# Attention over inducing points and a gated product in one kernel: coefficients without a clip, the first group of x in one load, and another order of all operations

## The chip, the cores and the metric

One Trainium2 chip, one core. The metric is the device time of one execution in microseconds (us). TensorE (PE) multiplies, VectorE (DVE) and ScalarE (ACT) read its results from PSUM and write to SBUF, GpSimd (POOL) works in SBUF and issues the loads that change the type, SyncE (SP) issues the other transfers.

## The reference

```python
# x: (4, 12480, 128), inducing: (32, 128), w_in: (128, 2048), w_out: (2048, 128)
def mab(q, kv):
    s = scale * (q @ kv.transpose(0, 2, 1))          # scale = 1 / sqrt(128)
    s = s - s.max(-1, keepdims=True)
    a = np.exp(s)
    a /= a.sum(-1, keepdims=True) + 1e-09
    return a @ kv
h = mab(I, x)                       # per batch: 32 rows out of 12480
y = mab(x, h)                       # per batch: 12480 rows, each a mixture of the 32 rows of h
u = y.reshape(49920, 128) @ w_in
out = (u * np.clip(u + 3.0, 0.0, 6.0) / 6.0) @ w_out
```

## The kernel before

Each row of y is a mixture of 32 rows of h, so u is a mixture of the 32 rows of h @ w_in, and, where no u leaves -3 to 3, the result is a quadratic form in the 32 weights. The kernel computes the coefficients of this form once for each batch and then needs, for each row of x, products of two weights with these coefficients. At the end a verdict is counted that the assumptions held; where it fails, a slow direct path runs. With these inputs it does not run.

A batch has six groups of 2048 rows (16 tiles of 128) and a small one of 192 rows. Everything up to the verdict is a list of short operations, written out by hand in one table, ORDER. A token there is an operation's code, then batch, group and details, and at the end often the PSUM bank and the engine (V, A or P for VectorE, ScalarE, POOL). The function runs through the tokens and issues the instructions of each on its engine. Engines and queues work in the order of the table, each for itself, and wait for each other where data or buffers demand it.

The operations that the text names:

- X loads a group of x (fp32 in HBM, fp16 in SBUF; issued by POOL; seven buffers xh). T transposes 8 tiles on TensorE, Y copies the result to SBUF (xT). S are the scores against the inducing rows, E their exponentials (a), A the sums over rows on TensorE, H adds them to hacc on VectorE.
- When hacc of a batch is complete: c3 spreads the denominator on TensorE, c4 inverts it, c9, cK, cA, cB make HS and Wd (h and differences of its rows), c7 and c8 split hacc in two bf16 parts, G multiplies by w_in on TensorE (w_in itself split in w_hi and w_lo by wh and wl), cG scales to GL. cD copies GL to Gd in bf16 (two halves). Then, for the coefficients of single weights, cH and cI, L with w_out, cL, cm and cN, cM; for the products of pairs, p (a 128x2048 product, PR) and P with w_out in bf16 (wb); cP, cX and cY bring the coefficients into place (Cq).
- For each group: Z are TensorE's products of xT with HS and Wd, Zz and Zd take them out of PSUM (z, and dk by an exponential), Ze makes e, ee its square, W spreads dk over partitions by a transfer from SBUF to SBUF (d, issued by SP). B spreads z to pairs on TensorE, F takes the exponential (TF, 128x1024), U multiplies TF by d (TD, 128x2048). R, Rr and R2 give the squared normalization. l and q are TensorE's products with the coefficients, v multiplies them by the normalization and writes os, O stores os to HBM (SP).
- wi and wo load w_in and w_out (POOL), i and w are constants and warm-up products at the start. y0 to y3 count for the verdict on VectorE (each count is a pass over a small tile at line 831), y4 sums over partitions on TensorE, y5 makes bad_i, and all engines read bad_i before they end. cJ takes the largest |GL| of a batch for the verdict (g_all), cC and cQ are sums of squares for it on ScalarE.

The lines that the profile names: 416 X, 422 T, 428 Y, 433 S, 441 E, 449 A, 459 A's denominators, 476 H, 481 c3, 402 wh, 405 wl, 532 cG, 540 cD, 543 cH, 548 cI, 553 cJ, 563 L, 609 p, 616 P, 641 cQ, 656 Z, 666 Zd, 671 Ze, 678 Zz, 692 ee, 698 W, 704 R, 731 B, 741 F, 750 U, 770 l, 789 q, 807 and 811 v, 817 O, 831 counts, 854 y4.

Of the kernel before, what the change touches and what calls it, by code (L numbers as in the profile page):

```python
# [183 lines left out]
def kernel(  # L184
# [35 lines left out]
    with ExitStack() as es:  # L220
# [321 lines left out]
        def op_cH(b, e):  # L542
            veng(e).tensor_scalar(
                r6[:, :, :], GL[:, :, :M].bitcast(FP32), 3.0, 0.0, op0=ALU.add, op1=ALU.max
            )
# [485 lines left out]
```

## Time and profile before

| | |
|---|---|
| time, median of 3 runs | 248.84 us (248.77 to 250.02) |
| time of the profiled execution | 249.51 us |
| its span, first to last instruction | 247.5 us |
| mean granted TensorE clock | 0.982 |
| busy: PE, DVE, ACT, POOL | 227.0, 202.4, 191.1, 40.3 us |
| moved by DMA | 53.91 MB |

How to read it: the busy time of an engine is the time in which it worked on an instruction; TensorE's matmuls overlap, so their durations are longer than their distance. The granted clock is the share of full speed that the throttle allowed to TensorE. In a list of groups a row has line, engine, operation, output<-input and count, then busy us and mean ns of one, then the idle time just before and what ended it. In a list of waits it is the engine and line that waited, what it waited for, the sum in us, the times and the longest. A row of the timeline starts with start and length in us. A row of the chain that ended last has start, length, engine, tile and line.

### The profile page before, as it was taken

What the parts mean: (1) busy time and instruction counts of PE and PEld (TensorE: products, weight loads), DVE (VectorE), ACT (ScalarE), POOL (GpSimd) and SP (SyncE); (2) the same over time, 40 slices, a digit from 0 to 9 for tenths busy, and PEclk for the clock granted to TensorE, in tenths of its full rate; (3) what the DMA queues carried; (4) which work ended last, traced back from release to release, by engine and by line L of the source; (5) the groups of instructions that cost most, each with busy time, mean ns of one, the idle gap of its engine ahead of it and who ended that gap; (6) DMA issues with size and microseconds to landing.
All of it is one profiled execution on the core that took longest, in us unless ns stands there. A gap on an engine that the chain in (4) does not pass through costs nothing. (4 is left out here: it accounts for less than half of the span.)

```text
span 247.5 us, 10076 instructions
## 1 busy us (share of the span) xinstructions
PE 227.0 (92%) x4317; PEld 186.5 (75%) x4317; DVE 202.4 (82%) x438; ACT 191.1 (77%) x350; POOL 40.3 (16%) x80
## 2 busy tenths in 40 slices
PE   1879799999799999999899999999999999989990
PEld 0568758888698798797787888888878877768780
DVE  0236879989599997999778998988889999998983
ACT  2167277998788886999687786999889889989870
POOL 8518582021002500010004000000031000000000
PEclk9999679999999999999999999999999999999998
DMA  6999789969989999849879974623981849696953
GB/s 96 193 255 254 238 158 193 208 163 250 214 286 263 277 196 331 293 87 250 184 252 265 266 274 110 224 56 76 338 305 37 262 97 340 211 311 170 362 232 134
DMA packets 23744, 53.91 MB, mean 218 GB/s; under 512 B 3697, under 2 KB 16785, under 8 KB 20753
## 3 DMA queue, kind: packets, MB, share of 16 engines
q1 hardware_dynamic: 19072, 38.36, 47.4%
q0 software_dynamic: 4624, 14.88, 31.0%
q8 instruction: 34, 0.56, 0.8%
q14 instruction: 14, 0.11, 0.1%
HBM read 27.67 MB, written 25.56 MB: 215 GB/s over the span
## 5 line engine op out<-in xcount | busy, mean ns | idle before, releaser
L741 ACT ACTIVATE TF<-ps 128x1024 f16<-128x1024 f32 (+1 forms) x100 | 96.8, 1007 | 16.1 <-PE ps L731 12.4
L750 DVE TENSOR_TENSOR TD<-TF,d 128x2048 f16<-128x2048 f16 (+1 forms) x52 | 59.9, 1156 | 3.0 <-ACT TF L741 2.2
L789 PE MATMUL ps<-Cq,TF 128*128 128x128 f16 (+1 forms) x784 | 57.9, 219 | 2.6 <-issue 1.4
L789 PE MATMUL ps<-Cq,TD 128*128 128x128 f16 (+1 forms) x784 | 56.0, 219 | 0.0
L807 DVE TENSOR_TENSOR os<-ps,r 128x512 f32<-128x512 f32 x68 | 45.4, 683 | 11.7 <-PE ps L789 4.1
L789 PEld LDWEIGHTS <-TF 128*128 128x128 f16 (+1 forms) x784 | 46.3, 98 | 6.3 <-issue 6.0
L789 PEld LDWEIGHTS <-TD 128*128 128x128 f16 (+1 forms) x784 | 46.1, 99 | 4.3 <-issue 3.4
L811 ACT ACTIVATE os<-ps,r 128x128 f32<-128x128 f32 x112 | 32.0, 380 | 4.3 <-PE ps L789 2.0
L422 PE MATMUL ps<-ident_h,xh 128*128 128x128 f16 x384 | 29.8, 226 | 5.5 <-DMA xh<-in_x_dram 5.5
L422 PEld LDWEIGHTS <-xh 128*128 128x128 f16 x384 | 24.0, 102 | 11.6 <-DMA xh<-in_x_dram 7.5
L428 DVE COPY xT<-ps 128x1024 f16<-128x1024 f16 x31 | 21.2, 684 | 12.8 <-PE ps L422 12.5
L428 ACT COPY xT<-ps 128x1024 f16<-128x1024 f16 x17 | 17.0, 1015 | 18.9 <-PE ps L422 18.8
L416 POOL DMA_DIRECT2D xh<-in_x_dram x25 | 13.9, 560 | 75.1 <-PE ps L459 62.2
L731 PE MATMUL ps<-z,pair 32*128 32x256 f16 (+1 forms) x400 | 20.3, 270 | 0.0
L609 DVE TENSOR_TENSOR PR<-Gd 128x2048 bf16<-128x2048 bf16 x16 | 19.8, 1239 | 0.0
L678 DVE TENSOR_SCALAR_CACHE_REDUCE z<-ps 128x512 f16<-128x512 f32 (+1 forms) x28 | 17.3, 621 | 2.4 <-PE ps L656 2.3
L666 ACT ACTIVATE dk<-ps 128x512 f16<-128x512 f32 (+1 forms) x28 | 14.8, 547 | 5.5 <-PE ps L656 3.4
L770 PE MATMUL ps<-BD,ee 64*128 64x256 f16 (+1 forms) x196 | 17.5, 273 | 0.2
L441 ACT ACTIVATE a<-ps 128x512 f16<-128x512 f32 (+1 forms) x27 | 14.6, 556 | 2.6 <-PE ps L433 2.6
L616 PE MATMUL ps<-w_ob,PR 128*128 128x128 bf16 x256 | 16.5, 219 | 0.0
L671 ACT ACTIVATE e<-z 128x512 f16<-128x512 f16 (+1 forms) x28 | 16.3, 589 | 0.1
L616 PEld LDWEIGHTS <-PR 128*128 128x128 bf16 x256 | 14.7, 98 | 0.9 <-issue 0.8
(137 smaller groups left out, 284.8 us busy)
## 6 DMA issues: line engine op xcount, KB each, us to landing
...
xh<-in_x_dram POOLq DMA_DIRECT2D x23, 512.0 KB, 8.8
os<-in_moe_w_in_dram POOLq DMA_DIRECT2D x2, 512.0 KB, 13.4
w_or<-in_moe_w_out_dram POOLq DMA_DIRECT2D x2, 512.0 KB, 11.6
out_dram<-os SPq DMA_DIRECT2D x2, 512.0 KB, 3.6
...
```

Of the source, the lines that this page charges most:

```text
L422: nc.tensor.transpose(pt[:, (i - lo) * p : (i - lo + 1) * p], at(xh, xhl, b, g)[:p, i, :], ident_h[:p, :p])
L428: copier(e)(xT_of(b, g)[:, lo * p : hi * p], ps[:, k, :].bitcast(FP16)[:, : (hi - lo) * p])
L609: veng(e).tensor_mul(pr_of(b, c)[:, :, :].rearrange("p a (i m) -> p a i m", m=M), views[0], views[1])
L616: nc.tensor.matmul(ps[:, k, f * C : (f + 1) * C], lhsT=pr_of(b, c)[:, jb, :], rhs=w_ob[:, jb, :], start=first_of(b, u), stop=False, skip_g ...
L678: nc.vector.tensor_scalar(fat(z_, b, g)[:rows, :w], ps[:rows, k, :w], 1.0, None, op0=ALU.mult, op1=ALU.min, accum_out=z_all[:rows, b * NGR ...
L731: nc.tensor.matmul(ps[:, pairs[j // 2] + j % 2, f * w : (f + 1) * w], lhsT=pair[rows, f, :], rhs=fat(z_, b, g)[rows, h * w : (h + 1) * w], ...
L741: nc.scalar.activation(hat(TF_, b, g, h)[:, 2 * q : 2 * q + 2, :w], ps[:, k : k + 2, :w], ACT.Exp, scale=scale / KH)
L750: nc.vector.tensor_mul(split(hat(TD_, b, g, h)), split(hat(TF_, b, g, h)), d.unsqueeze(2).to_broadcast([P, J, 2, w]),)
L770: nc.tensor.matmul(ps[:p, ks[jp], s2 * 2 * C : (s2 + 1) * 2 * C], lhsT=fat(e2_, b, g)[rows, s * p : (s + 1) * p], rhs=BD_[b % 2][rows, :, ...
L789: nc.tensor.matmul(ps[:p, k, (s2 * 2 + j2) * C : (s2 * 2 + j2 + 1) * C], lhsT=t[:, j, f * w + s2 * p : f * w + (s2 + 1) * p], rhs=Cq_[b % ...
L807: nc.vector.tensor_mul(o, src, r.unsqueeze(3).to_broadcast([p, Sh, 2, C]))
L811: nc.scalar.mul(o[:, s2, j2, :], src[:, s2, j2, :], r[:, s2, j2 : j2 + 1])
```

## The change

- cI no longer clips: cH (r6 = max(GL + 3, 0) on POOL) is gone, and cI computes (GL + 3) * GL in place of min(r6, 6) * GL. The two are the same where |GL| is at most 3, which the verdict demands.
- cJ moves from VectorE to ScalarE: a sum of the squares of GL in a partition and batch, with the bound 9 in y3 in place of the largest magnitude with the bound 3.
- Group 0 of batch 0 comes in one load (it came in two halves), and it is the first load.
- The table ORDER is another one: all operations stand in another order, and several change their engine. 13 of 28 squares ee and 3 of 16 products p go from VectorE to POOL. Of the copies Y, 23 run on ScalarE and 29 on VectorE (19 and 33 before). Eight warm-up products are left of sixteen. The count of z_all (y2) stands earlier, not among the last operations.

```diff
-        r6 = sb.tile([P, FB, M], FP32, name="r6")
...
-        def op_cH(b, e):
-            veng(e).tensor_scalar(
-                r6[:, :, :], GL[:, :, :M].bitcast(FP32), 3.0, 0.0, op0=ALU.add, op1=ALU.max
-            )
-
         def op_cI(b):
             nc.vector.scalar_tensor_tensor(
-                GL[:, :, M:], r6[:, :, :], 6.0, GL[:, :, :M].bitcast(FP32), op0=ALU.min, op1=ALU.mult
+                GL[:, :, M:],
+                GL[:, :, :M].bitcast(FP32),
+                3.0,
+                GL[:, :, :M].bitcast(FP32),
+                op0=ALU.add,
+                op1=ALU.mult,
             )
 
         def op_cJ(b):
-            nc.vector.tensor_reduce(
-                g_all[:, b : b + 1],
+            nc.scalar.activation(
+                junk[:, :].rearrange("p (a m) -> p a m", m=M),
                 GL[:, :, :M].bitcast(FP32),
-                axis=AX.XY,
-                op=ALU.max,
-                apply_absolute_value=True,
+                ACT.Square,
+                accum_out=g_all[:, b : b + 1],
             )
...
-            count(3, g_all[:, :], 3.0, ALU.is_le)
+            count(3, g_all[:, :], 9.0, ALU.is_le)
...
-it X.0.1.0.16 i2 i1 w.2.0 i3.V T.0.1.0.8.1 Y.0.1.0.8.1.V i0 w.2.5 w.2.2 X.0.0.8.16 T.0.0.8.16.1 w.2.7 Y.0.0.8.16.1.V
...
+X.0.0.0.16 i2 w.2.1 w.2.7 X.0.6.0.2 it i1 i8 i0 i4.1 i5.1.V w.2.0 X.0.1.0.16 w.2.0 i3.V T.0.6.0.2.2 T.0.0.0.8.3
...
```

Three places show the order. A row has the line (in the changed kernel two or three less than before), the operation, output<-input with the buffers' own numbers, and the size. First POOL, from the constants at the start to the loads of w_out; xh0 to xh6 are the buffers of x, os1 takes w_in, sel, a1l, z_all and r2 are constants. Before:

```order
L391 DMA os1_118<-in_moe_w_in_dram 128x1024
L416 DMA xh5_73<-in_x_dram 128x2048
L361 MEMSET a1l0_95 128x128
L361 MEMSET a1l1_96 128x128
L362 MEMSET z_all_166 128x28
L363 MEMSET r2_165 128x392
L416 DMA xhl0_75<-in_x_dram 96x256
L391 DMA os1_118<-in_moe_w_in_dram 128x1024
L416 DMA xh0_68<-in_x_dram 128x2048
L416 DMA xh6_74<-in_x_dram 128x2048
L395 DMA w_or_150<-in_moe_w_out_dram 128x1024 x2
```

And now:

```order
L377 MEMSET sel_155 64x640
L381 TENSOR_TENSOR sel_155<-I4_152 32x128 x4
L382 CAST sel_155<-I4_152 32x128
L414 DMA xh5_73<-in_x_dram 128x2048
L359 MEMSET a1l0_95 128x128
L359 MEMSET a1l1_96 128x128
L360 MEMSET z_all_165 128x28
L361 MEMSET r2_164 128x392
L414 DMA xh4_72<-in_x_dram 128x2048
L389 DMA os1_118<-in_moe_w_in_dram 128x1024 x2
L414 DMA xh0_68<-in_x_dram 128x2048
L414 DMA xh6_74<-in_x_dram 128x2048
```

Both halves of w_in now stand behind the last large group of batch 0 (xh4), the small group (xhl0) is the second load of all, and sel is made between the fourth and the fifth large load.

Second VectorE around the end of the first batch's sums: w_hi and w_lo are wh and wl, hacc is H, rD and d_all are c4. Before:

```order
L428 COPY xT5_82<-ps_67 128x1024
L476 TENSOR_TENSOR hacc0_134<-hacc0_134,ps_67 128x33 x2
L402 CAST w_hi_147<-os1_118 128x512 x2
L476 TENSOR_TENSOR hacc0_134<-hacc0_134,ps_67 128x33 x5
L405 TENSOR_TENSOR w_lo_148<-os1_118,w_hi_147 128x512
L490 CAST HTb_139<-hacc0_134 128x32
L493 TENSOR_TENSOR HTl_140<-hacc0_134,HTb_139 128x32
L486 RECIPROCAL rD_136<-ps_67 128x32
```

And now:

```order
L426 COPY xT4_81<-ps_67 128x1024
L400 CAST w_hi_146<-os1_118 128x512
L403 TENSOR_TENSOR w_lo_147<-os1_118,w_hi_146 128x512
L400 CAST w_hi_146<-os1_118 128x512
L474 TENSOR_TENSOR hacc0_134<-hacc0_134,ps_67 128x33 x7
L484 RECIPROCAL rD_136<-ps_67 128x32
L485 COPY d_all_167<-ps_67 128x32
L494 SCALAR_TENSOR_TENSOR HQ_137<-hacc0_134,rD_136 128x64
```

Of the conversions of w_in one w_hi, one w_lo and another w_hi stand ahead of the last seven additions; the two others are on ScalarE, and no conversion stands between the additions and rD.

Third POOL's last operations, in batches 2 and 3: Wd is cB, HTl is c8, r6 is cH, ee and PR are the squares and the products p. Before:

```order
L416 DMA xh6_74<-in_x_dram 128x2048
L416 DMA xh2_70<-in_x_dram 128x2048
L514 TENSOR_TENSOR Wd1_133<-HQ_137 128x32
L493 TENSOR_TENSOR HTl_140<-hacc1_135,HTb_139 128x32
L543 TENSOR_SCALAR r6_143<-GL_141 128x512
```

And now:

```order
L414 DMA xh6_74<-in_x_dram 128x2048
L689 TENSOR_TENSOR ee2_102<-e2_99 128x512
L689 TENSOR_TENSOR ee1_101<-e1_98 128x512
L689 TENSOR_TENSOR ee2_102<-e2_99 128x512
L512 TENSOR_TENSOR Wd1_133<-HQ_137 128x32
L689 TENSOR_TENSOR ee1_101<-e1_98 128x512
L606 TENSOR_TENSOR PR0_121<-Gd_142 128x2048
L606 TENSOR_TENSOR PR2_123<-Gd_142 128x2048
L689 TENSOR_TENSOR ee1_101<-e1_98 128x512
L689 TENSOR_TENSOR ee0_100<-e0_97 128x512 x2
L689 TENSOR_TENSOR ee1_101<-e1_98 128x512
L689 TENSOR_TENSOR ee2_102<-e2_99 128x512
```

The clip is gone, and behind the last load of x POOL now has nine squares and two products of pairs (p.3.0 into PR0, p.3.2 into PR2).

More of the change, by code (lines that the diff above doesn't have):

```diff
@@ new lines @@
+T.1.5.0.8.7 T.1.5.8.16.6 cY.0.0.3.A W.0.1.3 Y.1.4.8.16.4.A X.1.6.0.2 R.0.2.2 R2.0.1.V Rr.0.3.0 Y.1.5.0.8.7.A
+q.0.0.0.1.0.3 W.0.1.0 U.0.0.0 q.0.0.0.0.1.0 q.0.0.0.1.1.3 l.0.0.0.0.3 l.0.0.1.7.1 X.2.1.0.16 ee.0.3.P Y.1.5.8.16.6.V
+Zd.0.4.5 W.0.3.0 W.0.2.1 R2.0.0.V v.0.0.0.1.3.A Rr.0.2.2 T.1.6.0.2.4 Y.1.6.0.2.4.A q.0.0.1.0.1.7 U.0.1.0 q.0.0.0.0.0.0
+v.0.0.0.0.0.A T.1.2.8.16.6 q.0.0.1.1.0.1 W.0.2.2 B.0.1.1.2.4 F.0.1.1.1.4 F.0.1.1.0.2 v.0.0.1.1.1.V Y.1.2.8.16.6.V
+q.0.0.1.0.0.7 T.1.2.0.8.0 Y.1.2.0.8.0.V q.0.1.0.1.0.1 q.0.1.0.1.1.1 v.0.0.1.0.7.V R2.0.3.V ee.0.1.P W.0.3.3 U.0.1.1
@@ new lines @@
+B.0.3.1.2.6 O.0.0.0.16 Ze.0.5 l.0.2.0.5.4 v.0.2.0.1.4.V W.0.4.1 F.0.3.1.1.6 W.0.4.3 l.0.2.1.1.0 q.0.2.1.1.1.0
+q.0.2.1.0.0.1 q.0.2.1.0.1.1 S.1.4.0.16.6 F.0.3.1.0.2 X.2.6.0.2 v.0.2.0.0.5.V v.0.2.1.0.1.V U.0.3.0 E.1.4.0.16.6
+S.1.5.0.16.7 E.1.5.0.16.7 q.0.2.1.1.0.0 A.1.6.0.2.4 H.1.6.0.2.4 A.1.4.0.16.1 H.1.4.0.16.1 W.0.4.2 T.2.1.8.16.6
+A.1.5.0.16.4 v.0.2.1.1.0.A U.0.3.1 H.1.5.0.16.4 c7.1.V B.0.4.0.2.0 F.0.4.0.0.2 q.0.3.0.1.1.5 c3.1.4 q.0.3.0.0.0.7
+q.0.3.0.0.1.7 ee.0.4.V c4.1.4 Y.2.1.8.16.6.V W.0.5.0 c9.1 R.0.4.2 Rr.0.4.2 F.0.4.0.1.0 cK.1 q.0.3.0.1.0.5 W.0.4.0
@@ new lines @@
+U.0.4.0 l.0.3.1.6.4 l.0.3.0.7.5 c8.1.V B.0.4.1.0.2 cQ.0 F.0.4.1.1.2 R2.0.4.V X.2.0.0.16 O.0.1.0.16 v.0.3.0.0.7.V
+X.3.6.0.2 q.0.3.1.1.1.4 F.0.4.1.0.0 q.0.3.1.0.1.6 q.0.3.1.0.0.6 v.0.3.1.0.6.A v.0.3.0.1.5.V U.0.4.1 G.1.2.3 G.1.1.3
+q.0.3.1.1.0.4 G.1.3.3 v.0.3.1.1.4.A G.1.0.3 q.0.4.0.0.0.2 cG.1.3 T.2.0.0.8.6 X.2.4.0.16 cD.1.0.V Y.2.0.0.8.6.A
+q.0.4.0.0.1.2 cD.1.1.V T.2.0.8.16.3 B.0.5.0.4.0 F.0.5.0.1.0 cA.1 q.0.4.1.1.1.6 W.0.5.3 Y.2.0.8.16.3.V cI.1 q.0.4.1.1.0.6
+F.0.5.0.0.4 cB.1.P Z.1.1.1.7 Z.0.6.0.0 Zz.0.6.0 Z.1.0.0.1 Z.1.2.1.3 Zz.1.0.1 Z.1.0.1.0 l.0.4.0.2.4 W.0.5.2 W.0.5.1
@@ new lines @@
+l.1.0.1.0.6 v.1.0.0.1.1.V R.1.3.7 R2.1.1.V Rr.1.3.7 R2.1.3.V q.1.0.1.0.1.0 U.1.1.0 F.1.1.1.0.2 q.1.0.1.1.1.6
+q.1.0.1.1.0.6 q.1.0.1.0.0.0 O.0.5.0.16 B.1.2.0.2.4 v.1.0.1.1.6.V W.1.2.2 F.1.2.0.0.2 Z.1.4.0.1 Zz.1.4.1 ee.1.1.V
+S.2.3.0.16.6 S.2.4.0.16.7 v.1.0.1.0.0.V R.1.2.2 Rr.1.2.2 T.2.5.0.8.3 F.1.2.0.1.4 Ze.1.4 q.1.1.0.1.1.1 U.1.1.1
+q.1.1.0.1.0.1 E.2.3.0.16.6 Y.2.5.0.8.3.A q.1.1.0.0.0.0 A.2.6.0.2.6 W.1.3.0 q.1.1.0.0.1.0 H.2.6.0.2.6 l.1.1.0.0.1
+v.1.1.0.0.0.V v.1.1.0.1.1.V E.2.4.0.16.7 W.1.3.2 B.1.2.1.4.2 F.1.2.1.1.2 S.2.5.0.16.6 A.2.3.0.16.7 H.2.3.0.16.7
@@ new lines @@
+v.1.5.0.1.1.A R.2.0.1 v.1.5.0.0.6.A q.1.5.1.1.0.5 W.2.0.3 T.3.2.0.8.7 W.2.1.0 v.1.5.1.1.5.A P.2.2.6 Rr.2.0.1 B.1.6.0.2
+B.2.0.0.0.4 F.2.0.0.1.4 P.2.3.6 Y.3.2.0.8.7.V P.2.1.7 F.1.6.0.0.2 F.2.0.0.0.0 cm.2.4 cM.2.1.6 p.2.0.V cM.2.0.7
+B.2.0.1.2.0 F.2.0.1.1.0 cN.2.4 cP.2.1.6 W.2.1.3 F.2.0.1.0.2 R.2.1.4 Rr.2.1.4 P.2.0.7 T.3.3.8.16.6 Y.3.3.8.16.6.A
+S.3.2.0.16.5 E.3.2.0.16.5 U.2.0.0 Z.2.3.1.4 cP.2.0.7 U.1.6.0 Z.2.3.0.0 Zz.2.3.0 Ze.2.3 W.2.1.1 Z.2.4.1.1 Z.2.2.0.2
+W.2.1.2 Zd.2.4.1 Z.2.4.0.7 Zz.2.2.2 T.3.4.8.16.3 A.3.2.0.16.0 S.3.3.0.16.6 cX.2.0.5 O.1.4.0.16 Zd.2.3.4 E.3.3.0.16.6
@@ new lines @@
+v.2.0.1.0.0.V U.2.1.1 R2.2.2.V S.3.5.0.16.1 E.3.5.0.16.1 W.2.3.2 O.1.5.0.16 q.2.1.0.1.0.5 q.2.1.0.0.0.4 A.3.5.0.16.7
+H.3.5.0.16.7 R.2.4.1 Rr.2.4.1 F.2.2.0.1.2 W.2.2.1 R2.2.4.V v.2.1.0.0.4.A q.2.1.1.1.0.6 q.2.1.0.1.1.5 v.2.1.0.1.5.V
+B.2.2.1.0.2 F.2.2.1.1.2 W.2.2.2 q.2.1.1.0.0.7 W.2.2.0 U.2.2.0 q.2.1.1.1.1.6 F.2.2.1.0.0 O.2.0.0.16 A.3.4.0.16.4
+Z.2.5.1.5 Zd.2.5.5 H.3.4.0.16.4 l.2.1.1.7.6 v.2.1.1.1.6.V W.2.4.2 B.2.3.0.0.2 F.2.3.0.1.2 c7.3.V q.2.1.1.0.1.7
+v.2.1.1.0.7.V W.2.4.0 q.2.2.0.0.1.6 q.2.2.0.0.0.6 c8.3.V ee.2.2.P l.2.2.0.6.7 B.2.3.1.4.2 W.2.4.1 F.2.3.0.0.0 ee.2.4.V
@@ new lines @@
+W.3.0.3 W.3.2.3 U.3.0.0 W.3.2.0 P.3.2.0 y0 cX.3.0.1 F.3.0.1.1.6 P.3.3.0 cP.3.1.0 F.3.0.1.0.4 q.2.6.0.0.1.3 Z.3.3.0.6
+Zz.3.3.6 cY.3.0.1.A U.3.0.1 W.3.1.1 Z.3.3.1.7 Zd.3.3.7 q.3.0.0.0.0.2 cX.3.1.4 W.3.1.2 Ze.3.2 cY.3.1.4.A B.3.1.0.6.0
+F.3.1.0.1.0 l.2.6.0.3 ee.3.2.V v.2.6.0.0.3.V l.3.0.0.2.5 R.3.2.4 q.3.0.0.1.1.5 F.3.1.0.0.6 O.2.4.0.16 q.3.0.0.1.0.5
+q.3.0.0.0.1.2 R2.3.0.V v.3.0.0.1.5.V q.3.0.1.0.1.3 Rr.3.2.4 v.3.0.0.0.2.V B.3.1.1.6.0 W.3.1.0 W.3.1.3 U.3.1.0
+q.3.0.1.0.0.3 Ze.3.3 R.3.3.5 F.3.1.1.0.6 F.3.1.1.1.0 Rr.3.3.5 q.3.0.1.1.1.4 q.3.0.1.1.0.4 l.3.0.1.3.4 cJ.3 R2.3.3.V
@@ new lines @@
+Z.3.4.1.2 Zd.3.4.2 v.3.0.1.1.4.V v.3.0.1.0.3.V Z.3.4.0.5 Zz.3.4.5 B.3.2.0.6.0 F.3.2.0.1.0 U.3.1.1 F.3.2.0.0.6
+q.3.1.0.0.0.4 q.3.1.0.1.0.2 W.3.2.2 q.3.1.0.0.1.4 q.3.1.0.1.1.2 l.3.1.0.4.2 B.3.2.1.0.6 W.3.2.1 F.3.2.1.1.6 F.3.2.1.0.0
+Z.3.5.0.5 R2.3.2.V W.3.3.0 Ze.3.4 q.3.1.1.0.0.3 O.2.5.0.16 v.3.1.0.1.2.V q.3.1.1.1.1.2 v.3.1.0.0.4.V Zz.3.5.5
+q.3.1.1.1.0.2 l.3.2.0.5.4 l.3.1.1.3.2 B.3.3.0.6.0 q.3.1.1.0.1.3 U.3.2.0 F.3.3.0.0.6 F.3.3.0.1.0 q.3.2.0.1.1.4
+v.3.1.1.1.2.V q.3.2.0.1.0.4 O.3.0.0.16 q.3.2.0.0.1.5 v.3.1.1.0.3.V q.3.2.0.0.0.5 v.3.2.0.1.4.A U.3.2.1 B.3.3.1.6.2
@@ new lines @@
+q.3.4.0.0.1.0 W.3.5.1 v.3.3.1.0.2.V q.3.4.0.0.0.0 cC.3 ee.3.6.V v.3.3.1.1.3.V U.3.4.1 Ze.3.5 B.3.5.0.4.6 F.3.5.0.0.4
+l.3.4.0.0.1 O.3.2.0.16 v.3.4.0.0.0.V l.3.4.1.2.3 q.3.4.0.1.0.1 v.3.4.0.1.1.V W.3.5.0 q.3.4.1.1.1.3 F.3.5.0.1.6
+q.3.4.1.1.0.3 v.3.4.1.1.3.A q.3.4.1.0.1.2 R.3.5.6 B.3.5.1.4.0 q.3.4.1.0.0.2 W.3.5.3 W.3.6.0 Rr.3.5.6 R2.3.5.V
+q.3.5.0.0.0.7 q.3.5.0.1.0.3 W.3.5.2 U.3.5.0 F.3.5.1.0.4 q.3.5.1.0.0.6 O.2.6.0.2 v.3.4.1.0.2.V q.3.5.0.1.1.3 ee.3.5.P
+l.3.5.0.7.3 l.3.5.1.6.4 W.3.6.1 F.3.5.1.1.0 U.3.5.1 cQ.3 O.3.3.0.16 v.3.5.0.1.3.A B.3.6.0.0 q.3.5.0.0.1.7 F.3.6.0.0.0
@@ L153 @@
+v.3.5.0.0.7.V q.3.5.1.0.1.6 v.3.5.1.0.6.A U.3.6.0 q.3.5.1.1.1.4 q.3.5.1.1.0.4 v.3.5.1.1.4.V q.3.6.0.0.0.1 R.3.6.0
+q.3.6.0.0.1.1 O.3.4.0.16 O.3.5.0.8 Rr.3.6.0 R2.3.6.V y3 l.3.6.0.1 v.3.6.0.0.1.A y1 O.3.5.8.16 O.3.6.0.2 y4.5 y5.5
 """
```

214 lines of the change are left out of this document (83 added, 131 removed).

## The prediction

> **What bounds the kernel now.** I read the page first (busy shares, the chain that ended last), then busy time by stretches, then TensorE's waits, then the timeline of the first 50 us.
>
> ```profile
> PE 227.0 (92%) x4317; PEld 186.5 (75%) x4317; DVE 202.4 (82%) x438; ACT 191.1 (77%) x350; POOL 40.3 (16%) x80
> PE 17%; DMA 6%; SPq 3%; ACT 2%; DVE 2%; issue 1%; POOL 0%; ACTq 0%; DVEq 0%
> ```
>
> The reader is to see that TensorE has work nearly all the time, and that it leads the chain that ended last. So an operation that leaves VectorE or GpSimd is worth nothing unless TensorE waited for it. The stretches show where TensorE is not full:
>
> ```profile
> 0.00:5.00 5.00, 1.03 (x2) 0.13 (x2) 0.50 (x2) 1.28 (x1) 3.89 (x12) 1.00 0.52 75
> 5.00:10.00 5.00, 3.12 (x17) 1.66 (x18) 0.69 (x1) 0.00 (x0) 4.37 (x25) 1.00 1.03 179
> 10.00:15.00 5.00, 4.13 (x73) 3.24 (x71) 1.82 (x5) 2.33 (x3) 0.39 (x1) 1.00 1.08 216
> 15.00:20.00 5.00, 4.54 (x98) 3.63 (x95) 1.92 (x7) 2.98 (x6) 2.11 (x4) 1.00 1.04 260
> 20.00:25.00 5.00, 4.42 (x130) 4.17 (x128) 3.56 (x10) 4.53 (x8) 4.23 (x6) 1.00 1.08 266
> 25.00:30.00 5.00, 3.35 (x58) 3.19 (x55) 4.49 (x16) 0.73 (x3) 2.96 (x5) 0.70 0.92 276
> 30.00:35.00 5.00, 5.00 (x101) 3.31 (x97) 3.28 (x8) 3.46 (x6) 3.20 (x4) 0.61 0.73 123
> ```
>
> The columns are length, busy time of PE, PEld, DVE, ACT and POOL, the granted clock, the DMA share and GB/s. Up to 25 us the DMA engines are full (share 1.03 to 1.08); from 25 to 35 us TensorE has a gap and then a granted clock of 0.70 and 0.61. TensorE's own waits:
>
> ```profile
> PE ps L422 <- DMA xh<-in_x_dram: 5.5, 3, 4.3
> PE ps L854 <- DVE junk L831: 1.9, 1, 1.9
> PE ps L789 <- issue: 1.4, 1, 1.4
> PE ps L789 <- ACT dk L666: 1.1, 1, 1.1
> PE ps L704 <- DVE os L807: 1.1, 1, 1.1
> ```
>
> The first row is the start, the second the verdict at the end; the other three, 3.6 us together, are all that is long after 40 us. Around the end of the first batch's sums:
>
> ```profile
> 24.89 1.45 DVE L402 CAST w_hi<-os 128x512 bf16<-128x512 f32 x2
> 25.78 0.35 PE L449 MATMUL ps<-a,xh 128*128 128x32 f16 x8
> 26.26 1.35 DVE L476 TENSOR_TENSOR hacc<-hacc,ps 128x33 f32<-128x33 f32 x5
> 27.66 0.63 PE L481 MATMUL ps<-I,hacc 128*128 128x32 f32 x2 [1.50 <-DVE hacc L476]
> 32.11 1.93 POOL L543 TENSOR_SCALAR r<-GL 128x512 f32<-128x512 f32 x1 [1.80 <-DVE GL L532]
> 35.41 1.05 DVE L548 SCALAR_TENSOR_TENSOR GL<-r,GL 128x512 fp32r<-128x512 f32 x1
> 36.56 0.67 PE L563 MATMUL ps<-w_or,GL 128*64 128x128 f32 x8
> 47.38 1.05 PE L789 MATMUL ps<-Cq,TF 128*128 128x128 f16 x16
> ```
>
> TensorE had its last sum (A) done at about 26.2 us, but five additions (H) stood on VectorE behind two conversions of w_in, so c3 began at 27.66; the clip (r6) and its second half (line 548) put L at 36.56; the first output product (q) came at 47.38.
>
> **The change part by part.**
>
> ```profile
> xh<-in_x_dram POOLq DMA_DIRECT2D x23, 512.0 KB, 8.8
> L405 POOL TENSOR_TENSOR w_lo<-os,w_hi 128x512 bf16<-128x512 f32 x2 | 3.1, 1536 | 0.8 <-DVE w_hi L402 0.7
> L692 DVE TENSOR_TENSOR ee<-e 128x512 f16<-128x512 f16 x24 | 9.8, 413 | 0.3 <-PE ps L770 0.3
> L609 DVE TENSOR_TENSOR PR<-Gd 128x2048 bf16<-128x2048 bf16 x16 | 19.8, 1239 | 0.0
> L553 DVE TENSOR_REDUCE g_all<-GL 128x1 f32<-128x512 f32 x4 | 2.7, 665 | 0.0
> L641 ACT ACTIVATE junk<-Cp 128x512 f32<-128x512 f16 x4 | 2.5, 635 | 0.0
> L741 ACT ACTIVATE TF<-ps 128x1024 f16<-128x1024 f32 x96 | 94.9, 1028 | 15.4 <-PE ps L731 11.9 <-ACT os L811 1.4 <-PE ps L789 0.7
> L428 ACT COPY xT<-ps 128x1024 f16<-128x1024 f16 x17 | 17.0, 1015 | 18.9 <-PE ps L422 18.8
> L671 ACT ACTIVATE e<-z 128x512 f16<-128x512 f16 x24 | 15.2, 640 | 0.1
> L441 ACT ACTIVATE a<-ps 128x512 f16<-128x512 f32 x21 | 12.6, 604 | 2.2 <-PE ps L433 2.2
> L666 ACT ACTIVATE dk<-ps 128x512 f16<-128x512 f32 x24 | 14.1, 598 | 4.2 <-PE ps L656 3.4 <-ACT TF L741 0.6
> L402 ACT CAST w_hi<-os 128x512 bf16<-128x512 f32 x1 | 1.1, 1130 | 0.0
> ...
> 25.94 1.66 POOL L405 TENSOR_TENSOR w_lo<-os,w_hi 128x512 bf16<-128x512 f32 x1
> ```
>
> *First loads.* A group of x is 0.524 MB (the 512 KB of the first row); six and a small one make 3.19 MB. The GB/s column over stretches of 5 us adds up to 0.38, 1.27, 2.35, 3.65 and 4.98 MB by 5, 10, 15, 20 and 25 us. Before, one half of w_in stood ahead of the sixth group; now both halves stand behind all of x. So the last group should land at 15 us plus 0.84 MB at 260 to 216 GB/s: 18.2 to 18.9 us. The second half of w_in ends at 4.24 MB, 20 us plus 0.59 MB at 266 GB/s: 22.2 us, nearly as before. POOL now has the constants sel between its loads, but four groups, 2.1 MB, are issued ahead of them, and by the sums these keep the queue busy to about 14 us. Nothing is gained or lost there.
>
> *End of the first batch's sums.* Two gates. TensorE's: after the last landing come 16 transposes, a copy (1.02), scores, four half-size exponentials and the last sums with their additions; by the rows that is 5 to 6 us, so 23.6 to 24.6 us. VectorE's: one conversion of w_in now stands ahead of seven additions, instead of two ahead of the last five. 22.2 plus 0.73 (1.45 for two) plus seven additions at 0.27 (1.35 for five) is 24.8. I take c3 at 24.6, a lead of 3.1 us; the ends are 23.6 (both gates early) and 27.7 (the loads are no earlier).
>
> *No clip.* cI follows cG directly. In the first batch 3.3 us lay between the start of r6 and that of cI, so L could come earlier by that much and more. But then the exponentials of ScalarE set the first q: between c3 and the first q it has, in its new order, three copies (1.02), six TF (1.03), four e (0.64), four dk (0.60), three a (0.60), one conversion (1.13), the new sum of squares (0.64) and four small ones that I estimate at 0.5 each from the shorter forms above: 3.1 + 6.2 + 2.6 + 2.4 + 1.8 + 1.1 + 0.6 + 2.0 = 19.8 us. From 24.6 this is 44.4; with some waiting I take 44.8 against 47.38, so 2.6 us of the lead are left. In batches 1 to 3 the clip costs nothing before either, since q of the former batch fills TensorE (no wait for GL stands among its waits).
>
> *Clock.* From 25 to 35 us the gate took 0.30 and 0.39 of 5 us: 3.4 us of full clock at most, of which a filled TensorE loses about 2. After the change transposes and Z are there right behind c3, so the gap may be short enough. ScalarE's 19.8 us would then be the limit anyway: 0, with ends 0 and -2. The Trainium skill, "TensorE: Matmul & The Clock Gate", Part 1, has the clock fall after at least one idle window of about 3.4 us. Here it fell with TensorE busy 3.35 of 5 us, so by the trace the window need not be idle throughout; by the page no such fall would come in either kernel, and the sum would be the same.
>
> *Warm-up products.* Eight of sixteen go. While loads limit the start they cost nothing; with fewer of them the clock may open one window later. 0, with ends -1.5 and +1.
>
> *What moves between engines.* Thirteen squares (ee) and three products (p) go to POOL, and the check of the gate moves to ScalarE: VectorE loses 13 x 0.41 + 3 x 1.24 + 4 x 0.67 = 11.7 us, ScalarE gains 4 x 0.64 and four copies at 1.02, 6.6 us of some 56 us in which it is idle. Neither ended TensorE's waits often: 0. On POOL nothing of that kind was timed; the nearest row is w_lo, 1.54 us for 512 columns, so 1.5 us for ee and 6.2 us for p, with ends 1.0 (cheaper for 16-bit inputs) and 1.8, and 4 and 8. What covers a late p.3.0 is TensorE's other work between the later copy of Gd and P.3.0:
>
> ```profile
> 234.33 0.33 PE ps L731 x8
> 236.56 0.54 PE ps L770 x8
> 237.29 2.79 PE ps L789 x48
> ```
>
> Eleven q at 0.47 (2.79 for 48), five B at 0.33, two l at 0.54, with L and R some 8.5 us. 6.2 fits; if that cover were gone, P.3.0 would wait for the whole 6 us. The Trainium skill, "GPSIMD Engine Reference", 3.1 and 4.1, speaks against the move: elementwise work with two inputs is about half as fast there as on VectorE, and POOL shares its way to SBUF with VectorE. Its 4.5 us for 2048 fp32 columns would put p, as an estimate, below the 6.2 us taken here, and the sum would not move.
>
> *The tail.* One count of the verdict (z_all) leaves the stretch behind the last normalization:
>
> ```profile
> 242.56 0.18 DVE L831 TENSOR_SCALAR_CACHE_REDUCE junk<-z_all 128x28 f32<-128x28 f32 x1
> 242.78 0.26 DVE L831 TENSOR_SCALAR_CACHE_REDUCE junk<-r 128x98 f32<-128x98 f32 x1
> ```
>
> The next began 0.22 us later, so -0.2; the end is 0 if the last stores land later than the verdict.
>
> *Order after 45 us.* The three long waits of 3.6 us can go, and others can come; a new order of the same work says nothing on the sign. I take -0.5, with ends -3.6 and +3.6.
>
> Sum: -2.6 - 0.2 - 0.5 = -3.3. The profiled execution took 249.51 (its span is 247.5), so 246.2 for one like it; the median shown, 248.84, is 0.67 lower: 245.5.
>
> **The rivals.**
> - *More is gained.* The clock stays up (-2) and most of the 3.6 us of waits go: 248.84 - 2.6 - 0.2 - 1 - 2.5 = 242.5. For it speaks that TensorE has transposes and Z at once behind c3; against it, that ScalarE is full there.
> - *The lead is lost.* ScalarE, or transfers that have no gap now, hand the lead back by 60 us, and the order later is no better: 248.84 - 0.2 to -0.8, about 248.5. For it speaks that the DMA engines are already full (1.03 to 1.08) up to 25 us, and that the new order sends as much through them earlier. A part of this is that taking out the clip does not shorten anything, as in batches 1 to 3.
> - *Slower.* POOL's three products hold TensorE. If VectorE's use of SBUF stretches p to over 8.5 us, P.3.0, P.3.2 and P.1.1 each wait; at 10 us each wait is about 2, and the squares behind them come late too: +6 against -3.3, so 251.5. It decides from p above 8.5 us. Against it: the slower w_lo, beside a busy VectorE, took 1.66 us, which would be 6.6 for p.
>
> **How the numbers follow.** The forecast has 0.47 (its own range 244.0 to 247.4), more gained 0.19, the lead lost 0.20, slower 0.14. About 0.5%, 1.24 us, is what a measurement of this kernel can tell from no change: under 247.6 is faster, over 250.1 slower. So faster 0.66, same 0.20, slower 0.14. The range leaves out most of the slower case and the far end of the first rival: 242.5 to 250.0.
>
> **What would show it.** Right: c3 at 24 to 25 us, no addition of hacc late, the first q by 45.5 us, the verdict's counts one fewer, PR on POOL at 5 to 7 us with no wait of TensorE for it. Wrong: the last group of x landing after 21 us, a granted clock below 1 for longer than 7 us, or new waits over 1 us in the stretches from 60 us on.

## The result, and the profile after

The changed kernel takes 259.66 us (median of 4 runs, 259.12 to 260.5) against 249.43 for the kernel before on the same chip: ratio 1.042, 95% interval 1.037 to 1.047. It is slower by 4%, where 245.5 us and a gain of 1.3% were forecast. Some executions of these kernels run a few per cent longer than the others; the medians below hold them, the ratios with their intervals leave them out (so a ratio can differ from that of two medians), and the profiles of e9, e10 and e11 are of such executions.

The profiled execution took 259.12 us, its span is 257.1 us. First the page, the busy time and the engines' shares of the chain that ended last:

```profile
PE 232.4 (90%) x4309; PEld 193.5 (75%) x4309; DVE 200.2 (78%) x410; ACT 198.3 (77%) x366; POOL 59.9 (23%) x91
PE 58%; DMA 19%; DVE 9%; ACT 4%; POOL 3%; issue 3%; SPq 2%; DVEq 0%; ACTq 0%; POOLq 0%
```

TensorE issues eight matmuls fewer and is busy 5.4 us longer; three stretches of half clock, shown below, fit that. In the chain, transfers have 19% and VectorE 9%. The chain of the kernel before was followed over 31% of its span and this one over 98%, so their shares do not compare, and that TensorE led the former says little. The stretches (length, busy PE, PEld, DVE, ACT, POOL, granted clock, DMA share, GB/s) show where:

```profile
20.00:25.00 5.00, 4.29 (x131) 4.02 (x131) 3.54 (x9) 3.93 (x8) 1.68 (x2) 1.00 1.06 277
25.00:30.00 5.00, 3.27 (x34) 1.93 (x38) 3.85 (x10) 2.93 (x6) 2.94 (x5) 0.66 1.05 242
30.00:35.00 5.00, 5.00 (x110) 4.43 (x103) 3.90 (x8) 3.62 (x8) 3.00 (x6) 0.66 0.80 221
40.00:45.00 5.00, 3.17 (x48) 2.47 (x46) 3.98 (x6) 2.08 (x5) 0.00 (x0) 1.00 1.10 232
45.00:50.00 5.00, 3.21 (x34) 3.14 (x34) 2.00 (x4) 3.83 (x8) 0.00 (x0) 0.71 0.61 138
100.00:120.00 20.00, 18.24 (x336) 15.59 (x337) 17.05 (x38) 12.80 (x23) 1.98 (x2) 0.91 0.35 96
200.00:220.00 20.00, 17.57 (x270) 14.39 (x271) 17.56 (x32) 14.63 (x31) 4.34 (x3) 0.91 0.41 110
```

The gap and the half clock from 25 to 35 us stand as before. New are three places: 40 to 50 us, just after 100, and just after 200, each with less work of TensorE and a clock below 1. The list of waits names one for each, in the order of time the first, the third and the second row; the last row here is ScalarE's:

```profile
PE ps L701 <- ACT dk L663: 3.6, 1, 3.6
PE ps L786 <- DVE TD L747: 2.5, 1, 2.5
PE ps L613 <- DVE PR L606: 1.9, 1, 1.9
PE ps L851 <- DVE junk L828: 1.7, 1, 1.7
ACT dk L663 <- DMA d<-dk: 4.1, 1, 4.1
```

The timeline at the three places (start and length; in brackets the idle time before and what ended it), with c3 and the first q:

```profile
25.75 0.41 PE L479 MATMUL ps<-I,hacc 128*128 128x32 f32 x2 [0.80 <-DVE hacc L474]
46.15 0.60 ACT L663 ACTIVATE dk<-ps 128x512 f16<-128x512 f32 x1 [4.07 <-DMA d<-dk]
46.80 0.24 PE L701 MATMUL ps<-blk,e 128*128 128x4 f16 x4 [3.62 <-ACT dk L663]
51.42 0.61 PE L786 MATMUL ps<-Cq,TD 128*128 128x128 f16 x8
94.19 4.64 POOL L606 TENSOR_TENSOR PR<-Gd 128x2048 bf16<-128x2048 bf16 x1
95.90 4.08 DVE L606 TENSOR_TENSOR PR<-Gd 128x2048 bf16<-128x2048 bf16 x1
101.76 4.43 PE L613 MATMUL ps<-w_ob,PR 128*128 128x128 bf16 x48 [1.94 <-DVE PR L606]
192.95 8.31 POOL L606 TENSOR_TENSOR PR<-Gd 128x2048 bf16<-128x2048 bf16 x2
193.33 1.89 DVE L804 TENSOR_TENSOR os<-ps,r 128x512 f32<-128x512 f32 x3 [0.28 <-PE ps L786]
195.13 2.58 DVE L747 TENSOR_TENSOR TD<-TF,d 128x2048 f16<-128x2048 f16 x1
197.98 4.37 DVE L747 TENSOR_TENSOR TD<-TF,d 128x2048 f16<-128x2048 f16 x1
202.41 0.62 PE L786 MATMUL ps<-Cq,TD 128*128 128x128 f16 x8 [2.48 <-DVE TD L747]
```

Two things are to be seen. At 46 us ScalarE could not write the next dk, since its buffer was still being read by a transfer W, and so the first q came at 51.42 (47.38 before). At 95.90 and 197.98 an operation of VectorE that takes 1.2 us elsewhere took 4.08 and 4.37; it ended 1.1 us behind POOL's p (99.98 against 98.83, 202.35 against 201.26), as if it had begun only when POOL was done. Not all of VectorE's work is held: the three os at 193.33, which read one of their two inputs from PSUM, took 0.63 us each beside POOL's p, as elsewhere. Behind each of the three waits follow 3.4 us of half clock (from 47.1, 101.7 and 204.1 us); the second of them:

```profile
101.70:105.10 3.40, 3.34 (x32) 3.34 (x33) 3.34 (x6) 0.00 (x0) 0.00 (x0) 0.50 0.16 47
```

The account: 4.0 us later at the first q; 1.9 + 1.7 (half of 3.4, if TensorE has work all the time) at 100; 2.5 + 1.7 at 202. That is 11.8 us against 9.6 between the spans, so by this account the rest of the new order is some 2 us better than the old.

### The profile page after: what moved, and what is told of

The parts are those of the page before. It is cut to its first block, busy times and chain, and to the rows that moved or that the text cites. A ratio compares the mean times of both kernels' runs of the same rounds, so it can differ in the third digit from the quotient of the medians.

```text
span 257.1 us, 10076 instructions
## 1 busy us (share of the span) xinstructions
PE 232.4 (90%) x4309; PEld 193.5 (75%) x4309; DVE 200.2 (78%) x410; ACT 198.3 (77%) x366; POOL 59.9 (23%) x91
## 4 chain that ended last, share of the span: by engine, by line
PE 58%; DMA 19%; DVE 9%; ACT 4%; POOL 3%; issue 3%; SPq 2%; DVEq 0%; ACTq 0%; POOLq 0%
PE ps L786 26%; DMA out_dram<-os 11%; PE ps L613 7%; PE ps L728 5%; PE ps L420 4%; DMA d<-dk 4%; PE ps L767 4%; DMA xh<-in_x_dram 4%; PE ps L653 4%; PE ps L447 3%; PE ps L431 3%; DVE TD L747 2%; DVE os L804 2%; DVE PR L606 2%; SPq L695 2%
## 5 line engine op out<-in xcount | busy, mean ns | idle before, releaser
L738 ACT ACTIVATE TF<-ps 128x1024 f16<-128x1024 f32 (+1 forms) x100 | 95.6, 1008 | 20.2 <-PE ps L728 17.6
L747 DVE TENSOR_TENSOR TD<-TF,d 128x2048 f16<-128x2048 f16 (+1 forms) x52 | 65.3, 1255 | 2.4 <-ACT TF L738 1.4
L786 PE MATMUL ps<-Cq,TD 128*128 128x128 f16 (+1 forms) x784 | 57.2, 220 | 2.5 <-DVE TD L747 2.5
L689 POOL TENSOR_TENSOR ee<-e 128x512 f16<-128x512 f16 x13 | 17.3, 1336 | 107.9 <-PE ps L767 57.5
L420 PE MATMUL ps<-ident_h,xh 128*128 128x128 f16 x384 | 30.6, 235 | 3.0 <-DMA xh<-in_x_dram 3.0
L420 PEld LDWEIGHTS <-xh 128*128 128x128 f16 x384 | 25.4, 106 | 4.5 <-DMA xh<-in_x_dram 3.6
L426 DVE COPY xT<-ps 128x1024 f16<-128x1024 f16 x27 | 18.1, 684 | 7.8 <-PE ps L420 7.2
L426 ACT COPY xT<-ps 128x1024 f16<-128x1024 f16 x21 | 21.0, 1016 | 2.1 <-PE ps L420 1.9
L613 PE MATMUL ps<-w_ob,PR 128*128 128x128 bf16 x256 | 20.4, 249 | 1.9 <-DVE PR L606 1.9
L613 PEld LDWEIGHTS <-PR 128*128 128x128 bf16 x256 | 18.7, 115 | 2.6 <-DVE PR L606 2.0
```

What stands on the lines that cost most here:

```text
L420: nc.tensor.transpose(pt[:, (i - lo) * p : (i - lo + 1) * p], at(xh, xhl, b, g)[:p, i, :], ident_h[:p, :p])
L426: copier(e)(xT_of(b, g)[:, lo * p : hi * p], ps[:, k, :].bitcast(FP16)[:, : (hi - lo) * p])
L613: nc.tensor.matmul(ps[:, k, f * C : (f + 1) * C], lhsT=pr_of(b, c)[:, jb, :], rhs=w_ob[:, jb, :], start=first_of(b, u), stop=False, skip_g ...
L689: veng(e).tensor_mul(fat(e2_, b, g)[:rows, :w], e_in, e_in)
L738: nc.scalar.activation(hat(TF_, b, g, h)[:, 2 * q : 2 * q + 2, :w], ps[:, k : k + 2, :w], ACT.Exp, scale=scale / KH)
L747: nc.vector.tensor_mul(split(hat(TD_, b, g, h)), split(hat(TF_, b, g, h)), d.unsqueeze(2).to_broadcast([P, J, 2, w]),)
```

## The experiments

**Two causes, one at a time.** e1 gives VectorE the three products back, e2 lets W.0.0.1 go ahead of two other transfers on SP, e3 does both:

```diff
-p.1.1.P ... p.3.0.P ... p.3.2.P
+p.1.1.V ... p.3.0.V ... p.3.2.V
```

```diff
-W.0.1.1 L.0.0.7 W.0.1.2 ... P.0.3.7 W.0.0.1
+W.0.0.1 W.0.1.1 L.0.0.7 W.0.1.2 ... P.0.3.7
```

> The changed kernel with its three products of pairs on POOL (p.1.1, p.3.0, p.3.2) back on VectorE, in the same places of the order; nothing else. Theory SBUF (a product of two inputs on POOL holds up VectorE operations with two 16-bit inputs from SBUF until it ends): the TD of 4.4 and 2.6 us and the PR of 4.1 us at 94 to 100 and 193 to 202 us go back to about 1.2, TensorE's waits of 1.9 and 2.5 us and the half clock behind them go; 6 to 9 us less than the changed kernel, 251 to 254. Rival theory (the new order alone costs the time, through transfers that come later): less than 2 us gained.

> The changed kernel with one transfer moved: W.0.0.1 stands before W.0.1.1 and W.0.1.2 on SP's queue, fourth and not sixth. Theory queue order (the sixth transfer falls behind loads of x that are issued at 33 us; Zd.0.3 waits for its buffer, R.0.1 and P behind it): TensorE's wait of 3.6 us at 42.8 to 46.8 us and the half clock behind it go, 3 to 5 us less than the changed kernel. Rival (the loads of x slow all transfers of that stretch, whatever their order): the wait moves to W.0.1 and d of the second group, under 1.5 us gained.

> Both edits together, the three products back on VectorE and W.0.0.1 first. If the two causes are independent their gains add: 9 to 13 us less than the changed kernel, 247 to 251, which is about the kernel before. If one of them only uncovers the next wait, less than 7 us.

Measured, against 250.26 us for the kernel before: e1 254.79 us, ratio 1.026 (1.018 to 1.033); e2 252.48, 1.016 (1.007 to 1.025); e3 249.16, 1.001 (0.996 to 1.006). Each takes away its part and leaves the other. In e1 the waits of 2.5 and 1.9 are gone (one of 1.2, for a p on VectorE, is new at 200.6 us), and the wait at 45 us has grown to 4.5, so that the first q comes at 52.91; e1 gained 4.9 us, less than the 6 to 9 expected. In e2 the first q comes at 46.9 us and the two waits of 2.5 and 1.9 are there. e2 gained 7.2 us, more than the 3 to 5 expected: 4.6 us at the first q, and in its profile the wait of 2.5 us is followed by full clock (1.00 from 198 to 206 us), which is not the edit's doing. Together the two causes make up the whole loss, but none of the forecast gain is left.

**The products in the kernel before.** e4 moves the same three to POOL there, and nothing else:

```diff
-p.1.1.V ... p.3.0.V ... p.3.2.V
+p.1.1.P ... p.3.0.P ... p.3.2.P
```

> The kernel before with the same three products of pairs (p.1.1, p.3.0, p.3.2) moved from VectorE to POOL in its own order; nothing else. Theory SBUF: each takes 4 to 5 us on POOL, VectorE's TD and PR beside it stretch to 2.5 to 4.4 us, TensorE waits; 4 to 10 us slower than before. Rival (POOL's work costs nothing of its own, the order of the changed kernel does): within 1.5 us of before.

260.93 us (257.89 to 262.32 in 4 runs, too few for an interval), against 250.26: at least some 8 us more by three products alone. TensorE's longest waits for VectorE are 2.1, 2.2 and 2.8 us there, for an os behind cI, for HS and for TD, which took 3.67 (cI), 3.17 (HS) and 4.76 us (TD). In its timeline cI, an fp32 product of two operands in SBUF that took 1.05 us before, is held in the same way, and ends 0.5 us behind POOL:

```profile
84.33 4.89 POOL L611 TENSOR_TENSOR PR<-Gd 128x2048 bf16<-128x2048 bf16 x1 [2.56 <-DVE Gd L542]
86.09 3.67 DVE L550 SCALAR_TENSOR_TENSOR GL<-r,GL 128x512 fp32r<-128x512 f32 x1
```

**Why W.0.0.1 was late.** Two readings: its place among SP's transfers, or the loads of x that share the DMA engines with it. Transfers of dk in a window of similar work (queue, count, KB each, median us from issue to landing), in the changed kernel from 33 to 46 us and in the kernel before from 29 to 40:

```profile
d<-dk SPq DMA_DIRECT2D x6, 128.0 KB, 11.0
```

```profile
d<-dk SPq DMA_DIRECT2D x10, 128.0 KB, 4.2
```

e8 leaves SP's order and issues three of the five loads later:

```diff
-X.1.2.0.16 ... X.1.6.0.2 ... X.2.1.0.16 ee.0.3.P
+... ee.0.3.P X.1.2.0.16 X.1.6.0.2 X.2.1.0.16
```

> The changed kernel with only three loads moved: X.1.2, X.1.6 and X.2.1 are issued behind the square ee.0.3 on POOL, so after about 44 us instead of at 35.8 to 38.8 us; the order of SP's own queue, with W.0.0.1 sixth, stays. Theory (W.0.0.1 landed 10 us after its issue because loads of x were in flight on the DMA engines): it lands at 38 to 40 us behind the two loads that are left, ScalarE's dk waits under 1.5 us for it instead of 4.1, TensorE's wait of 3.6 us and the half clock at 47 to 50.5 us go, time 254 to 257 instead of 259.7 (less of a gain than with W moved, as the three loads then arrive late for their transposes). Rival (the place in SP's own queue is what made it late, whatever x does): the wait stays at 3 to 4 us and the time at 259 or more.

265.91 us, ratio 1.060 (1.052 to 1.068): the time went the other way, but the wait in question answers. ScalarE's longest wait for a transfer of dk is 1.6 us instead of 4.1, and TensorE's behind it 1.1 instead of 3.6:

```profile
ACT dk L665 <- DMA d<-dk: 2.2, 2, 1.6
PE ps L703 <- ACT dk L665: 1.1, 1, 1.1
```

By the profile's time from issue to landing, W.0.0.1 was issued at 34.88 us in the changed kernel and landed 11.2 us later, at 46.0; in e8, issued at 36.67, it took 7.7 us, and in e2, issued at 33.81 beside the two loads of 33.72 and 34.29, 7.9 us. So both readings have a part. Three loads less in flight took 3.5 us off the transfer in the same place of SP's order; a place two transfers earlier took as much off with all loads there. The theory of e8 had more: landing at 38 to 40 us, where it was 44.4, and a part of the shorter wait is that ScalarE came 0.8 us later to it. What the run lost stands later: the square ee.0.3 came at 52.10 us, not at 44, so the three loads were later than meant, and TensorE waited 8.1 us for the small group of the second batch.

**A third case of the same kind at the start.** In the changed kernel one w_lo runs on POOL while VectorE makes HQ, on which HS and Wd and so the first Z wait:

```profile
26.54 1.40 POOL L403 TENSOR_TENSOR w_lo<-os,w_hi 128x512 bf16<-128x512 f32 x1
26.66 1.38 DVE L494 SCALAR_TENSOR_TENSOR HQ<-hacc,rD 128x64 f32<-128x64 f32 x1
```

e5 is e3 with this w_lo on VectorE:

```diff
-wl.0.V Zz.0.0.3 ... wl.3.P
+wl.0.V wl.3.V Zz.0.0.3 ...
```

> The changed kernel with the three products back on VectorE, with W.0.0.1 ahead of W.0.1.1, and with the last second half of w_in (w_lo, a 128x512 subtraction in fp32) on VectorE, behind the other one there, instead of on POOL. Theory (POOL's two-input work in SBUF holds VectorE's): HQ, which took 1.38 us beside that subtraction, takes about 0.2 us again; the first Z starts 0.9 to 1.1 us earlier than with the same kernel and the subtraction on POOL (28.3 us there), the half clock of that stretch becomes shorter, and the time falls by 0.5 to 1.5 us from 249.2 us. Rival (HQ was long for another reason, such as its own operands): HQ stays at 1.2 to 1.4 us and the time stays within 0.5 us, or rises as VectorE has 1.1 us more to do.

246.95 us (245.26 to 249.53), ratio 0.989 (0.985 to 0.993): with these repairs the changed kernel is 1.1% faster than the kernel before, and more is gained over e3 than the 0.5 to 1.5 us expected. HQ is short again. The first Z came only 0.4 us earlier (27.95), not 0.9 to 1.1, as TensorE was busy until then with 16 transposes at half clock (from 26.12 us); but the half clock ended sooner (1.00 from 30 to 35 us, 0.81 in e3), L, which needs the products G, came 2.1 us earlier than in e3, and the first q at 44.51 (46.60 in e3). The half clock did not become shorter, as the theory had it: it lasts 6.8 us in both, from 25.1 us in e3 and from 22.3 in e5. How much of the 2.1 us is HQ's, and how much is where the half clock fell, one profile of each does not tell; the gain in time is shown. The first row here is of e5, the other two of e3 and e5, L:

```profile
26.81 0.23 DVE L496 SCALAR_TENSOR_TENSOR HQ<-hacc,rD 128x64 f32<-128x64 f32 x1
```

```profile
37.68 0.70 PE L562 MATMUL ps<-w_or,GL 128*64 128x128 f32 x8
```

```profile
35.61 0.69 PE L562 MATMUL ps<-w_or,GL 128*64 128x128 f32 x8
```

**The squares.** e6 is e3 with all 13 squares on VectorE:

```diff
-ee.0.3.P ... (13 of them)
+ee.0.3.V ...
```

> The changed kernel with the three products back on VectorE, with W.0.0.1 ahead of W.0.1.1, and with all 13 squares ee that went to POOL back on VectorE: POOL then has no work with two inputs beyond the start. Theory 1 (POOL's use of SBUF holds VectorE whatever the size): 13 holds of up to 1 us go, VectorE's two-input operations at those places are short again, 13 x 0.41 us come to VectorE; time lower by 0.5 to 2 us than the 249.2 us with the squares on POOL. Theory 2 (short POOL operations fall into VectorE's gaps and only relieve it): time the same within 0.7 us or up to 2 us higher, since VectorE gains 5.4 us of work.

251.54 us, ratio 1.008 (1.003 to 1.013) against 1.001 (0.996 to 1.006) of e3: some 1.7 us more by the ratios, whose intervals overlap. That speaks against the first theory and for the second, at its upper end. TensorE now waits for a square on VectorE (1.3 us in two waits, none in e3). POOL's squares took 1.2 us each in e3; that they are a gain is likely, but not clear of the noise.

**The clock at the start.** e10 and e12 are e5 with warm-up products in TensorE's waits; e10 has four, three, four and four, e12 only the last two groups:

```diff
-... T.0.6.0.2.2 ... T.0.1.0.8.2 ... T.0.4.0.8.3 ... c3.0.5
+... w.4.2 T.0.6.0.2.2 ... w.3.2 T.0.1.0.8.2 ... w.4.3 T.0.4.0.8.3 ... w.4.5 c3.0.5
```

> The changed kernel with the three products and the w_lo on VectorE and W.0.0.1 ahead, as above (246.95 us), and 15 warm-up products more, placed in TensorE's waits of the first 26 us: 4 ahead of the transposes of the small group, 3 ahead of those of the second group, 4 ahead of those of the last group that lands, 4 ahead of c3. Theory (half clock at 8 to 13 us and at 22 to 28 us followed from those waits): the granted clock stays at 1.00 from 10 to 30 us or falls for one window instead of two; the first q starts 1 to 2 us earlier than at 44.5 us; time 245 to 246. Rival (up to 26 us the loads set the pace, and the products only stand ahead of the real ones): c3 at 25.5 to 26.5 us as before, the first q at 44 to 45.5, time 246.5 to 248.

> The changed kernel with the three products and the w_lo on VectorE and W.0.0.1 ahead, and 8 warm-up products more, only in the two waits of TensorE at 19 to 20 and 24.7 to 25.7 us. Theory (the half clock from 22 to 28 us costs the first coefficients): the clock is 1.00 from 15 to 30 us, the first q 0.5 to 1 us earlier than at 44.5 us, time 245.5 to 246.5. Rival (VectorE and ScalarE set that stretch, as with 15 products more, where the clock stayed at 1.00 and the first q came at 44.3): first q at 44.2 to 44.8 us, time 246.5 to 247.5.

e10: 249.68 us, ratio 0.984 (0.977 to 0.991, from three executions); e12: 247.77 us, 0.989 (0.985 to 0.993). Neither can be told from e5. In e12 the clock is up from 15.6 us on, where e5 has half clock from 22.3 to 29.2, and the first q still comes at 44.33:

```profile
25.00:30.00 5.00, 4.35 (x68) 2.66 (x65) 4.12 (x13) 4.46 (x7) 1.78 (x4) 1.00 1.07 244
30.00:35.00 5.00, 4.67 (x132) 4.12 (x135) 4.88 (x13) 4.37 (x9) 2.72 (x5) 1.00 0.90 280
44.33 0.61 PE L788 MATMUL ps<-Cq,TD 128*128 128x128 f16 x8
```

The rivals hold: the half clock at that place costs no more than 0.2 us at the first q. That VectorE (busy for 4.9 of the 5 us) and ScalarE set this stretch fits the rows, but was not tried by itself.

**The clip alone.** e7 is the kernel before without the clip, cI right behind cG, the check of GL as in the change:

```diff
-cG.0.2 ... cH.0.P ... cI.0
+cG.0.2 cI.0
-cH.1.P ... cH.2.P ... cH.3.P
```

> The kernel before, with nothing changed but the clip: cH is left out, cI computes (GL + 3) * GL right behind cG, and the sum of squares of GL for the verdict is on ScalarE with the bound 9. Theory 1 (the clip did not set the first L, since L began without a wait in the kernel before): L of the first batch still starts at 36 to 37 us, the first q at 46.5 to 47.5, time within 0.7 us of the kernel before (250.3 us). Theory 2 (the clip's 3.3 us stood in the chain to the coefficients): L and the first q come 1 to 3 us earlier, time 248 to 249.

256.51 us, ratio 1.026 (1.021 to 1.031). The head is as the second theory has it: L at 34.82 us (36.56 before), the first q at 45.62 (47.38), of which 0.5 us is an earlier c3 (27.13). And yet the kernel is 6 us slower, which neither theory had. It is lost at 143 us:

```profile
ACT os L811 <- DMA out_dram<-os: 5.5, 1, 5.5
PE ps L731 <- ACT os L811: 3.9, 1, 3.9
```

There are two buffers os; ScalarE waited for a store, and 3.4 us of half clock follow behind TensorE's wait. e9 moves the store O.1.3 ahead on SP:

```diff
-W.2.0.2 ... W.2.0.1 ... O.1.3.0.16
+O.1.3.0.16 ... W.2.0.2 ... W.2.0.1
```

> The kernel before without the clip, as above, and one store moved: O.1.3, which SP issued at 138.55 us behind two transfers W of the next batch that wait for their dk, goes ahead of them, behind W.1.6.1. Theory (the 1.8 us won at the first q were lost to the two os buffers: ScalarE and VectorE could not write the next output before O.1.3 had landed): the waits of 5.5 and 3.1 us for that store and TensorE's 3.9 us at 143.7 go; time 248 to 250 us, at least 4 us below the 256.5 us without the move. Rival (SP's place is not it, the DMA engines are simply full with loads of x there): the store still lands after 141 us, the waits stay over 2 us, time 254 or more.

255.38 us, ratio 1.017 (1.011 to 1.024), with TensorE's wait still 3.6 us: my theory fell. That store was not the one. In e7 the one before it, O.1.2, issued at 128.78, landed only after 142, 13.6 us later, and POOL's queue shows what was in flight beside it. Before:

```profile
131.24 1.92 POOL L543 TENSOR_SCALAR r<-GL 128x512 f32<-128x512 f32 x1 [2.76 <-DVE r L723]
133.12 1.15 POOL L416 DMA_DIRECT2D xh<-in_x_dram  x2
```

And in e7:

```profile
127.72 1.10 POOL L417 DMA_DIRECT2D xh<-in_x_dram  x2
```

The clip's cH waited on POOL for GL (the row names the operation of VectorE that ended just before), and two loads of x waited behind it. Without it they go 5.4 us earlier, 1.1 us ahead of the store. e11 is e7 with cH of the third batch put back, its result unused:

```diff
-cK.2 R.1.5.5
+cK.2 cH.2.P R.1.5.5
```

> The kernel before without the clip, with one operation of it put back: cH of the third batch runs on POOL in its old place, and nothing reads its result. Theory (cH also held back the two loads of x that stand behind it on POOL's queue: issued at 133.12 us in the kernel before, at 127.72 us without the clip, where they ran into the store O.1.2): the two loads are issued at 130 to 132 us, ScalarE's wait of 5.5 us and TensorE's of 3.9 us for the os buffers go, and the first batch's lead of 1.8 us stays: 247.5 to 250 us, 1 to 2 us under the kernel before on the same chip. Rival (the loss has another cause): the waits stay over 2 us, and the time at 254 to 257 us.

252.72 us, ratio 1.0045 (1.0002 to 1.0088). ScalarE's wait for the store is gone, and of the 2.6% of e7 2.2 points are back: the gate was worth more than what the clip cost. The 1.8 us of the lead do not show at the end, though, and the 1 to 2 us under the kernel before that were expected did not come. In the profile of e11 VectorE waits up to 4.6 us for another store, and TensorE 4.0 us behind it until 82.7 us. Whether the lead goes there or elsewhere stays open.

## Why the prediction was wrong

- *First loads and c3.* c3 came at 25.75 us, a lead of 1.9, not 3.1. TensorE waited for the last group until 20.2 us, where 18.2 to 18.9 was taken: the sum let all bytes of x go ahead of those of w_in, but by 20 us 3.6 MB had moved, of which x is 3.2. C3's lead was mis-sized by 1.2 us.
- *No clip, and the first q at 44.8.* That L would come earlier was right (1.2 us in e7 beyond c3's shift). **The first q is a step that failed:** it came at 51.42, 4.0 us later than before and not 2.6 earlier. The list of ScalarE's work held no wait for a transfer, and "some waiting" was 0.4 us; ScalarE waited 4.1 us for the buffer that W.0.0.1 was reading. Nor does the list of 19.8 us set the first q elsewhere: from c3 to the first q it took 19.7 before, 18.5 in e7, 18.8 in e5, 20.9 in e3 and 25.7 in the changed kernel. In e3 HQ stood behind POOL, and then came the last w_lo and G.
- *Clock and warm-up products: 0.* Nothing contradicts them. The half clock stayed (0.66 and 0.66). In the repaired kernel, where it lay at 22.3 to 29.2 us, taking it away gained nothing measurable (e12); for its place in the changed kernel, 26.6 to 33.4 us, that was not tried.
- *What moves between engines: 0.* **This is a step that failed.** It priced p on POOL by how long P can wait for it. The estimate was even too high (4.3 us each on average, not 6.2), and P never waited for POOL. It left out that VectorE's work with two inputs in SBUF stands still while POOL's p runs: "Neither ended TensorE's waits often" was read from a profile in which POOL had next to nothing with two inputs. e1 puts the price at 4 to 5 us, e4 at more. The squares alone, put at 0, seem to gain some 1.7 us (e6).
- *Order after 45 us: -0.5, ends ±3.6.* **The second step that failed,** together with the first q. The new order put W.0.0.1 sixth on SP, while POOL's queue issued loads of x from 33 us on, where it had a pause before. That loads and transfers W share the DMA engines was said for the start and nowhere after it. Its price is 4.6 us at the first q (51.42 against 46.9 in e2) and 6 to 7 us in time, beyond the end given.
- *Tail: -0.2.* Right: 1.7 us at the verdict instead of 1.9.
- *Rivals.* The slower one named the right three products, but decided "from p above 8.5 us" on POOL; it was decided at 4.6 us, by what VectorE could not do meanwhile. The lead lost named "transfers that have no gap now", which is what befell W.0.0.1, and priced them at the lead alone. With the three faults (the products, W.0.0.1, the w_lo on POOL) repaired, e5 is 1.1% faster (0.7 to 1.5), where the sum said 1.3%. That these agree is in part luck: c3's lead was 1.2 us smaller than taken, and the squares, which seem to gain, stood at 0.

The rule that would have told it stands in the Trainium skill, "SBUF — State Buffer", section "Who interferes with whom": an operation of VectorE with two inputs in SBUF and one of POOL that reads SBUF need the same pair of ports, and whoever starts first keeps it for the whole instruction. The traces agree: 4.08, 4.37, 3.67 and 1.38 us against 1.2, 1.2, 1.05 and 0.23, each ending 0.1 to 1.2 us behind POOL's. The prediction cited another page of the Trainium skill, on speed and sharing, and took the sharing for a slower p.
